# Attention backward on one core: two PSUM copies exchanged between ScalarE and VectorE

## The chip, the core and the metric

The kernel runs on one core of a Trainium2 chip. The metric is the device time of one execution in microseconds (us); less is better. The time before is 1711.55 us, the median of seven runs that lie between 1707.64 and 1726.95 us.

Five engines of the core work side by side, each through its own instructions in order: TensorE (PE; loading its weights is shown apart as PEld), VectorE (DVE), ScalarE (ACT), GpSimd (POOL) and SyncE (SP), which here only starts transfers. Matmul results land in PSUM, from which VectorE and ScalarE copy them to SBUF, the working memory.

## The reference

Two independent attention blocks, A and B, of the same shape; the kernel gives the forward output and all gradients of both.

```python
B, Sq, D = 8, 96, 640
H, Sk, Dh = 32, 512, 128
def _A_ref(x, k_cache, v_cache, wq, wo):
    q = (x @ wq).reshape(B, Sq, H, Dh).transpose(0, 2, 1, 3)
    scores = jnp.einsum("bhqd,bhkd->bhqk", q, k_cache) * (Dh ** -0.5)
    p = _softmax(scores, axis=-1)
    o = jnp.einsum("bhqk,bhkd->bhqd", p, v_cache)
    return o.transpose(0, 2, 1, 3).reshape(B, Sq, H * Dh) @ wo
...
out, vjp = jax.vjp(forward, A_x, A_k_cache, A_v_cache, A_wq, A_wo, B_x, ...)
return (out, *vjp(grad_out))
```

So for each block there are the output and dx, dK, dV, dwq and dwo. All tensors are bf16. One gradient matters here: dwo of a head is the head's attention output O, tokens by 128, transposed, times grad_out, tokens by 640, summed over all 768 tokens (8 batches of 96).

## The kernel before

There are 2 x 32 heads of 8 batches each: 512 steps of one head and one batch, called ticks here. A class `Emitter` collects small functions with a tick and a slot within the tick, sorts them and emits them in that order, so that the stages of several batches and heads are interleaved. A scheduler below it then arranges the instructions on each engine by its own estimates and by priorities, and puts in the waits; the order on an engine can therefore change when an instruction changes its engine. All PSUM tiles come from one pool of eight banks (`bank`, tag "bank"): a new tile waits until the tile that last held its bank has been read.

In a tick the pipeline holds several batches at different stages. In the order of the chain for one batch:

- c_s2a: scores S_ps = Q K^T (L298, TensorE) and their negative row maximum negm (L300, VectorE).
- c_s2b: E_sb = exp(S - max) with the row sums (L310, ScalarE; the read of the sums is an instruction of its own, ACTIVATION_READ_ACCUMULATOR).
- c_s3a, c_s3b: rinv (L320, VectorE) and P_sb (L329, POOL).
- c_s45: the transposes of P (L365), the O matmuls (L359), and the copies PT_sb (L378) and OD (L375), both ScalarE. OD holds O and dQ, transposed, for some heads.
- c_s4: dV_ps (L389) and its copy (L392, ScalarE).
- c_s5b, c_s6: prod (L407, POOL), dP_ps (L417), dl_ps (L419), and dS_sb (L421, VectorE), which reads both PSUM tiles.
- c_s7: dK_ps (L432) and its copy (L435, ScalarE).
- c_s8: the dQ matmuls (L340), which share a PSUM tile x_ps with the O matmuls, and the transposes of dS (L346) with the copy dST_sb (L348, VectorE).
- In half the ticks K is transposed on TensorE (kT_ps L285) and copied by VectorE (KT_pe L287).

In every eighth tick, and spread over its neighbours, stands the work of a head. Ahead of a head: pB (transposes of wo and wq), pC (Q and dO projections, L243), pD (the same in token order, n_ps L258, copied as Qnat_h and dOnat_h). Behind a head, ten ticks and more after it: qA(h, 1) brings dQ to token order, qA(h, 0) brings O to token order, qB makes dwo in two halves of 320 columns, and qD makes dwq for two heads together. gU adds a group's share to the output and to dx (o_ps L512).

The table HK gives the ticks: within a head's schedule qA1 stands at 17, qA0 at 18, and the halves of qB at 19 and 20. The table EV (L47) names the engine of each head-level copy, "act" for ScalarE or "dve" for VectorE; evac (L155) turns the name into an instruction, whose line in the profile is L157 on ScalarE and L160 (L162 with a scale) on VectorE. The change concerns the copies at the ends of qA and qB:

```python
# qA, which == 0
n_ps = bank([128, 8 * 128], BF16, "nat_ps")
for i in range(nt):
    nc.tensor.transpose(n_ps[:, i * 128:(i + 1) * 128], src[...], ident[:])
evac(EV["qA%d" % which], dst[...], n_ps[:, 0:nt * 128]...)
# qB
w_ps = bank([128, w], F32, "dwo_ps")
for t in range(TT):
    nc.tensor.matmul(w_ps[:], Onat[:, t, :], S["g_nat"][:, t, c0:c0 + w], ...)
evac(EV["qB%d" % di], dwo_sb[:, c0:c0 + w], w_ps[:])
```

Onat (the copy of O in token order, 128 x 768 in bf16) and dwo_sb (128 x 640 in bf16) have one buffer each. After the second half, dwo_sb is stored by a DMA that POOL issues (L474; in the last head SP).

Of the kernel before, what the change touches and what calls it, by code (L numbers as in the profile page):

```python
# [43 lines left out]

OFF = dict(ldk=-5, ldv=-3, kt=-3, vt=0, s2=3, s3=3, s4=4, s5=5, s6=6, s7=7, s8=8)
HK = dict(pA=-10, pA2=-9, pB=-3, pC0=[-2, 0], pC1=[-1, 0], pD1=1, pD0=2, qA0=18, qA1=17, qB=[19, 20], qD=[(18, 0, 2), (19, 2, 4), (21, 4, 5)])
EV = dict(pB0="act", pB1="dve", pC00="act", pC01="act", pC10="act", pC11="dve", pD0="dve", pD1="dve", qA0="dve", qA1="dve", qB0="act", qB1="act", qD="dve", gU="act")  # L47
GSPREAD0 = 9
PRIO_OFF = 2000
GSPREAD1 = 9  # L50
# [3 lines left out]
def build_block(tc, em, tick0, blk, x, kc, vc, wq, wo, g_all, out_all, dx, dk, dv, dwq, dwo, ident, ones, pools, HG=6, first=True, groups=None):  # L54
# [100 lines left out]
    def evac(eng, dst, src, sc=None):  # L155
        if eng == "act":
            nc.scalar.activation(dst, src, ACT.Identity, scale=(1.0 if sc is None else sc))  # L157
        else:
            if sc is None:
                nc.vector.tensor_copy(dst, src)  # L160
            else:
                nc.vector.tensor_scalar(dst, src, float(sc), None, op0=ALU.mult)  # L162
# [42 lines left out]
    def pB(h):  # L205
        def f():
# [4 lines left out]
            woT_h = hd.tile([128, DC * 128], BF16, name="woT_h", bufs=1)  # L211
            evac(EV["pB0"], woT_h[:], woT_ps[:])
            st["woT_h"] = woT_h
# [3 lines left out]
            wqT_h = hst.tile([128, D], BF16, name="wqT_h")  # L217
            evac(EV["pB1"], wqT_h[:], wqT_ps[:])
            st["wqT_h"] = wqT_h
# [7 lines left out]
    def pC(h, which, si):  # L227
        def f():
# [13 lines left out]
            for c in range(DC):  # L242
                nc.tensor.matmul(q_ps[:], lhs(c), rhsT[:, c, t0:t0 + w], start=(c == 0), stop=(c == DC - 1))  # L243
            evac(EV["pC%d%d" % (which, si)], dst[:, t0:t0 + w], q_ps[:], sc)
        return f

    def pD(h, which):
        def f():
# [4 lines left out]
            for b0 in range(0, B, 8):  # L253
                nb = min(8, B - b0)
                n_ps = bank([Sq, 8 * 128], BF16, "n_ps")
                for i in range(nb):
                    b = b0 + i
                    nc.tensor.transpose(n_ps[:, i * 128:(i + 1) * 128], src[:, b * Sq:(b + 1) * Sq], ident[:])  # L258
                evac(EV["pD%d" % which], dst[:, b0 * 128:(b0 + nb) * 128], n_ps[:, 0:nb * 128])
        return f  # L260
# [177 lines left out]
    def qA(h, which):  # L438
        def f():
# [11 lines left out]
            for t0 in range(0, TT, 8):  # L451
                nt = min(8, TT - t0)
                n_ps = bank([128, 8 * 128], BF16, "nat_ps")
                for i in range(nt):
                    nc.tensor.transpose(n_ps[:, i * 128:(i + 1) * 128], src[:, (t0 + i) * 128:(t0 + i + 1) * 128], ident[:])  # L455
                evac(EV["qA%d" % which], dst[:, t0:t0 + nt, :], n_ps[:, 0:nt * 128].rearrange("p (t d) -> p t d", d=128))
        return f

    def qB(h, di):
        def f():  # L460
# [8 lines left out]
            for t in range(TT):  # L469
                nc.tensor.matmul(w_ps[:], Onat[:, t, :], S["g_nat"][:, t, c0:c0 + w], start=(t == 0), stop=(t == TT - 1))  # L470
            evac(EV["qB%d" % di], dwo_sb[:, c0:c0 + w], w_ps[:])
            st["dwo_n"] += 1
# [269 lines left out]
```

## Time and profile before

| | |
|---|---|
| median of seven runs | 1711.55 us |
| the profiled execution | 1708.54 us |
| its span, first to last instruction | 1706.7 us |
| mean granted TensorE clock | 0.995 |
| DMA share, mean rate | nine tenths or more in most slices, 248 GB/s |

The profile shows one execution. "Busy" is the time in which an engine works on an instruction; a wait shows as idle time before an instruction, with the engine or transfer that ended it. Matmuls overlap in TensorE's pipeline and their ends are modelled, so that TensorE's busy time is not a measure of how dense its work is.

The load on the engines differs between the ticks of a head. The table shows busy time in four neighbouring ticks, cut at the starts of S_ps, around the copies of one head (its Onat copy starts at 311.48 us):

| stretch, us | length | VectorE busy | ScalarE busy | what of the head lies in it |
|---|---|---|---|---|
| 307.42 to 310.09 | 2.67 | 2.67 | 2.52 | dQnat, dOnat_h copies (VectorE) |
| 310.09 to 313.22 | 3.13 | 3.13 | 2.49 | Onat, Qnat_h copies (VectorE) |
| 313.22 to 315.21 | 1.99 | 1.59 | 1.69 | first dwo copy (ScalarE) |
| 315.21 to 318.02 | 2.81 | 1.71 | 2.81 | second dwo copy (ScalarE) |

The longest waits over the whole run: P_sb on POOL for rinv of VectorE 572.9 us, E_sb on ScalarE for negm of VectorE 206.1, rinv on VectorE for E_sb of ScalarE 121.1, dK_sb on ScalarE for dK_ps of TensorE 62.6. Idle time of an engine that nobody waits for costs nothing.

### The profile page before, as it was taken

How to read it: one execution, taken by the hardware profiler on the slowest of the kernel's cores; microseconds unless marked ns; L12 is line 12 of the kernel's file. 1: busy time of each engine (PE TensorE's matmuls, PEld its weight loads, DVE VectorE, ACT ScalarE, POOL GpSimd, SP SyncE). 2: the span in 40 equal slices, each digit the busy share in tenths (PEclk: the TensorE clock that was granted, in tenths of full speed). 3: DMA queues.
4: the chain of work that ended last, by engine and by line, in shares of the span. 5: the costliest groups of instructions: out<-in, count | busy, mean ns of one | idle time of the engine just before them, and what ended most of it. 6: DMA issues, size and time to landing. Idle time of an engine off the chain costs nothing.

```text
span 1706.7 us, 56912 instructions
## 1 busy us (share of the span) xinstructions
PE 1682.9 (99%) x22008; PEld 1347.3 (79%) x22008; DVE 1323.5 (78%) x3048; ACT 1383.5 (81%) x3518; POOL 1040.0 (61%) x1747
## 2 busy tenths in 40 slices
PE   8989999999999999999899999999999999999999
PEld 6878778778778778778778877887788778778876
DVE  6877678878788778788778876787788778778877
ACT  7988789868869869869668997997799679868974
POOL 4766566656647647657466765675566557656754
PEclk9999999999999999999899999999999999999999
DMA  9999999989989999989999999999999999999994
GB/s 265 259 243 257 257 226 290 261 205 251 273 204 268 267 216 273 265 215 239 273 255 267 284 250 247 251 260 252 216 271 249 255 225 267 252 235 237 271 237 138
DMA packets 602543, 423.58 MB, mean 248 GB/s; under 512 B 421472, under 2 KB 560096, under 8 KB 602272
## 3 DMA queue, kind: packets, MB, share of 16 engines
q1 hardware_dynamic: 548688, 242.60, 71.4%
q0 software_dynamic: 53584, 177.35, 32.3%
q8 instruction: 172, 2.82, 0.7%
q14 instruction: 99, 0.81, 0.1%
HBM read 161.09 MB, written 159.12 MB: 188 GB/s over the span
## 4 chain that ended last, share of the span: by engine, by line
PE 92%; DMA 2%; ACT 2%; DVE 1%; issue 1%; POOL 0%; SPq 0%; DVEq 0%; ACTq 0%; POOLq 0%
PE o_ps L512 12%; PE q_ps L243 12%; PE dwo_ps L470 6%; PE dV_ps L389 6%; PE dK_ps L432 6%; PE dP_ps L417 6%; PE S_ps L298 6%; PE dwq_ps L490 6%; PE x_ps L340 5%; PE x_ps L365 5%; PE dst_ps L346 5%; PE x_ps L359 5%; PE kT_ps L285 3%; PE n_ps L258 3%; PE nat_ps L455 3%
## 5 line engine op out<-in xcount | busy, mean ns | idle before, releaser
L329 POOL TENSOR_SCALAR P_sb<-E_sb,rinv 96x512 bf16<-96x512 bf16 x512 | 352.3, 688 | 581.1 <-DVE rinv L320 572.9
L310 ACT ACTIVATE E_sb<-S_ps,negm 96x512 bf16<-96x512 f32 x512 | 356.4, 696 | 211.1 <-DVE negm L300 206.1
L421 DVE SCALAR_TENSOR_TENSOR dS_sb<-dP_ps,dl_ps,P_sb 96x512 bf16<-96x512 f32 x512 | 382.9, 748 | 64.1 <-PE dl_ps L419 48.1
L300 DVE TENSOR_REDUCE negm<-S_ps 96x1 f32<-96x512 f32 x512 | 347.5, 679 | 54.2 <-PE S_ps L298 51.3
L435 ACT ACTIVATE dK_sb<-dK_ps 128x512 bf16<-128x512 f32 x512 | 308.2, 602 | 68.9 <-PE dK_ps L432 62.6
L392 ACT ACTIVATE dV_sb<-dV_ps 128x512 bf16<-128x512 f32 x512 | 317.3, 620 | 0.0
L378 ACT ACTIVATE PT_sb<-x_ps 128x384 bf16<-128x384 bf16 x512 | 258.9, 506 | 0.0
L512 PEld LDWEIGHTS <-OD 128*128 128x128 bf16 x1536 | 132.2, 98 | 99.6
L398 POOL DMA_DIRECT2D out_dram<-dV_sb x256 | 194.9, 761 | 11.7 <-issue 8.3
L398 POOL DMA_DIRECT2D out_dram<-dK_sb x256 | 195.0, 762 | 8.8 <-issue 4.5
L389 PE MATMUL dV_ps<-dOnat_h,P_sb 96*128 96x128 bf16 x2048 | 198.6, 219 | 0.8 <-DVE dOnat_h L160 0.6
L432 PE MATMUL dK_ps<-Qnat_h,dS_sb 96*128 96x128 bf16 x2048 | 198.3, 219 | 0.0
L417 PE MATMUL dP_ps<-VT,dOT_h 128*96 128x512 bf16 x512 | 196.6, 384 | 1.7 <-DMA VT<-V_sb 1.7
L407 POOL TENSOR_TENSOR prod<-OD,dOT_h 128x96 bf16<-128x96 bf16 x512 | 184.0, 359 | 13.8 <-ACT OD L375 12.6
L348 DVE COPY dST_sb<-dst_ps 128x384 bf16<-128x384 bf16 x512 | 177.2, 346 | 7.4 <-PE dst_ps L346 6.1
L320 DVE RECIPROCAL rinv<-rowsum 96x1 f32<-96x1 f32 x512 | 79.5, 155 | 127.3 <-ACT E_sb L310 121.1
L375 ACT ACTIVATE OD<-x_ps 128x192 bf16<-128x192 f32 (+1 forms) x515 | 173.7, 337 | 4.0 <-PE x_ps L340 3.8
L365 PE MATMUL x_ps<-ident,P_sb 96*128 96x96 bf16 x2048 | 172.3, 205 | 1.2 <-POOL P_sb L329 0.8
L346 PE MATMUL dst_ps<-ident,dS_sb 96*128 96x96 bf16 x2048 | 172.4, 206 | 0.5 <-DVE dS_sb L421 0.5
L359 PE MATMUL x_ps<-PT_sb,V_sb 128*128 128x96 bf16 x2048 | 172.4, 206 | 0.4 <-ACT PT_sb L378 0.4
L340 PE MATMUL x_ps<-dST_sb,K_sb 128*128 128x96 bf16 x2048 | 171.0, 206 | 0.4 <-ACT PT_sb L378 0.4
L340 PEld LDWEIGHTS <-K_sb 128*128 128x128 bf16 x2048 | 131.8, 98 | 24.8 <-issue 0.8
(83 smaller groups left out, 3728.7 us busy)
## 6 DMA issues: line engine op xcount, KB each, us to landing
out_dram<-dV_sb POOLq DMA_DIRECT2D x256, 256.0 KB, 5.1
out_dram<-dK_sb POOLq DMA_DIRECT2D x256, 256.0 KB, 5.3
K_sb<-in_A_k_cache_dram SPq DMA_DIRECT2D x128, 256.0 KB, 4.9
V_sb<-in_A_v_cache_dram SPq DMA_DIRECT2D x128, 256.0 KB, 4.8
K_sb<-in_B_k_cache_dram SPq DMA_DIRECT2D x128, 256.0 KB, 5.3
V_sb<-in_B_v_cache_dram SPq DMA_DIRECT2D x128, 256.0 KB, 4.9
out_dram<-dwo_sb POOLq DMA_DIRECT2D x63, 160.0 KB, 4.9
out_dram<-dwq_sb POOLq DMA_DIRECT2D x31, 320.0 KB, 5.6
```

The lines of the kernel that those rows point to most:

```text
L300: nc.vector.tensor_reduce(negm[:], S_ps[:], axis=AX.X, op=ALU.max, negate=True)
L310: nc.scalar.activation(E_sb[:], st["S_ps"][:], ACT.Exp, bias=st["negm"][:], scale=1.0, accum_out=rowsum[:])
L329: pinned(nc.gpsimd.tensor_scalar(P_sb[:], st["E_sb"][:], st["rinv"][:], 0.0, op0=ALU.mult, op1=ALU.add))
L340: nc.tensor.matmul(dQT_ps, st["K_sb"][:, c, :], st["dST_sb"][:, c * Sq:(c + 1) * Sq], start=(c == 0), stop=(c == KC - 1))
L389: nc.tensor.matmul(dV_ps[:, c * 128:(c + 1) * 128], P_sb[:, c * 128:(c + 1) * 128], hs["dOnat_h"][:, b * 128:(b + 1) * 128], start=True, s ...
L392: nc.scalar.activation(SB[(blk, h, b // 2, "v")][:, b % 2], dV_ps[:], ACT.Identity, scale=1.0)
L398: pinned(nc.gpsimd.dma_start(dst[b - 1:b + 1, h].rearrange("b (p c) d -> p b (c d)", c=KC), SB.pop((blk, h, b // 2, which))[:]))
L417: nc.tensor.matmul(dP_ps[:], hs["dOT_h"][:, tok], st["VT"], start=True, stop=True)
L421: nc.vector.scalar_tensor_tensor(dS_sb[:], dP_ps[:], dl_ps[:, 0:1], st["P_sb"][:], op0=ALU.subtract, op1=ALU.mult)
L432: nc.tensor.matmul(dK_ps[:, c * 128:(c + 1) * 128], dS_sb[:, c * 128:(c + 1) * 128], hs["Qnat_h"][:, b * 128:(b + 1) * 128], start=True, s ...
L435: nc.scalar.activation(SB[(blk, h, b // 2, "k")][:, b % 2], dK_ps[:], ACT.Identity, scale=1.0)
L512: nc.tensor.matmul(o_ps[:], src[:, t * 128:(t + 1) * 128], rhs, start=(hh == 0), stop=(hh == groups[g] - 1))
```

## The change

Two entries of the table EV change. The copy of O in token order, qA0, goes from VectorE to ScalarE; the copy of the second half of dwo, qB1, goes from ScalarE to VectorE. Each is made 64 times, once per head. Computation, tiles, buffers and transfers stay.

```diff
-EV = dict(pB0="act", ..., qA0="dve", qA1="dve", qB0="act", qB1="act", qD="dve", gU="act")
+EV = dict(pB0="act", ..., qA0="act", qA1="dve", qB0="act", qB1="dve", qD="dve", gU="act")
```

More of the change, by code (lines that the diff above doesn't have):

```diff
@@ L46 @@
 HK = dict(pA=-10, pA2=-9, pB=-3, pC0=[-2, 0], pC1=[-1, 0], pD1=1, pD0=2, qA0=18, qA1=17, qB=[19, 20], qD=[(18, 0, 2), (19, 2, 4), (21, 4, 5)])
-EV = dict(pB0="act", pB1="dve", pC00="act", pC01="act", pC10="act", pC11="dve", pD0="dve", pD1="dve", qA0="dve", qA1="dve", qB0="act", qB1="act", qD="dve", gU="act")
+EV = dict(pB0="act", pB1="dve", pC00="act", pC01="act", pC10="act", pC11="dve", pD0="dve", pD1="dve", qA0="act", qA1="dve", qB0="act", qB1="dve", qD="dve", gU="act")
 GSPREAD0 = 9
```

## The prediction

> **What bounds the kernel now.** First the page, for the engine that is busiest and for the chain that ended last; then the groups with their shapes, for the price of a copy on either engine; then the timeline of one head on ScalarE, VectorE and TensorE.
>
> ```profile
> PE 1682.9 (99%) x22008; PEld 1347.3 (79%) x22008; DVE 1323.5 (78%) x3048; ACT 1383.5 (81%) x3518; POOL 1040.0 (61%) x1747
> ...
> PE 92%; DMA 2%; ACT 2%; DVE 1%; issue 1%; POOL 0%; SPq 0%; DVEq 0%; ACTq 0%; POOLq 0%
> ```
>
> TensorE is the wall: 99% busy, and 92% of the chain runs over it. No copy costs time by itself; it costs only where TensorE waits for it. But 99% hides small stalls, because the ends of matmuls are modelled and cover the gap behind them. So I read the starts. Undisturbed, successive matmuls of the same width start a fixed step apart (in the timeline 42 ns for 96 columns, 56 for 128, 136 for 320, 216 for 512). Each start-to-start gap of all 22,008 matmuls, less that step for the earlier one, gives **about 68 us of stall** over 1701 us. That is all that any evacuation edit can win. Cut at the starts of S_ps (L298), which gives eight ticks per head, four stalls above 60 ns recur at fixed places: dwo_ps (L470) in 25 heads, 4.6 us; dl_ps (L419) just before it in 21 heads, 3.8 us; the P transposes (x_ps L365) two ticks later in 23 heads, 3.5 us; the dQ matmuls (x_ps L340) one tick on in 23 heads, 3.9 us. **Sum 15.8 us.** One such head, the one whose O copy starts at 311.48 us, shows all four. TensorE:
>
> ```profile
> 312.08 0.42 PE L417 MATMUL dP_ps<-VT,dOT_h 128*96 128x512 bf16 x1
> 312.48 0.16 PE L419 MATMUL dl_ps<-ones,prod 128*96 128x1 bf16 x1
> 312.68 0.70 PE L470 MATMUL dwo_ps<-g_nat,Onat 128*128 128x320 bf16 x4
> ```
>
> A 512-column matmul should be followed after 0.22 us; dl_ps comes after 0.40 (0.185 late), dwo_ps after another 0.20 where 0.03 would do (0.167 late). Who ended just then stands in VectorE's and ScalarE's rows:
>
> ```profile
> 310.88 0.68 DVE L300 TENSOR_REDUCE negm<-S_ps 96x1 f32<-96x512 f32 x1
> 311.48 0.55 DVE L160 COPY Onat<-nat_ps 128x768 bf16<-128x768 bf16 x1
> 311.94 0.68 DVE L160 COPY Qnat_h<-n_ps 96x1024 bf16<-96x1024 bf16 x1
> ...
> 318.00 0.16 DVE L320 RECIPROCAL rinv<-rowsum 96x1 f32<-96x1 f32 x1 [0.99 <-ACT E_sb L310]
> ```
>
> ```profile
> 310.42 0.60 ACT L392 ACTIVATE dV_sb<-dV_ps 128x512 bf16<-128x512 f32 x1
> 311.66 0.68 ACT L310 ACTIVATE E_sb<-S_ps,negm 96x512 bf16<-96x512 f32 x1 [0.64 <-DVE negm L300]
> 312.24 0.19 ACT L310 ACTIVATION_READ_ACCUMULATOR E_sb<-S_ps,negm 96x1 f32 x1
> ...
> 316.86 0.45 ACT L157 ACTIVATE dwo_sb<-dwo_ps 128x320 bf16<-128x320 f32 x1
> 317.17 0.70 ACT L310 ACTIVATE E_sb<-S_ps,negm 96x512 bf16<-96x512 f32 x1
> ```
>
> dl_ps starts 0.05 us after the accumulator read ends (312.43): it waits for the PSUM bank of the scores. dwo_ps starts 0.06 after Qnat ends (312.62): the bank of n_ps. And Qnat is late because Onat stands in front of it, in a stretch of VectorE without one gap from 307.9 to 314.5, in which ScalarE idles 0.64 us. Later it is the other way round: at 316.86 the second dwo copy holds E_sb, whose negm ended at 316.73, while VectorE idles 0.99 us for it. The other two stalls hang on that: x_ps L365 starts at 316.99 just after P_sb lands (0.143 late), x_ps L340 at 318.89 just after dS_sb (0.161 late), both downstream of late E_sb.
>
> **Part by part.** The prices come from the nearest groups:
>
> ```profile
> L378 ACT ACTIVATE PT_sb<-x_ps 128x384 bf16<-128x384 bf16 x512 | 258.9, 506 | 0.0
> L157 ACT ACTIVATE woT_h<-woT_ps 128x640 bf16<-128x640 bf16 x64 | 46.5, 726 | 0.0
> L157 ACT ACTIVATE dwo_sb<-dwo_ps 128x320 bf16<-128x320 f32 x128 | 56.5, 442 | 4.6 <-PE dwo_ps L470 1.9
> ...
> L160 DVE COPY Onat<-nat_ps 128x768 bf16<-128x768 bf16 x64 | 34.8, 544 | 0.0
> L162 DVE TENSOR_SCALAR dwq_sb<-dwq_ps 128x512 bf16<-128x512 f32 x64 | 44.0, 688 | 30.3 <-PE dwq_ps L490 30.3
> L160 DVE CAST dOT_h<-q_ps 128x256 bf16<-128x256 f32 x64 | 26.6, 415 | 7.8 <-PE q_ps L243 7.8
> ```
>
> *Onat on ScalarE.* Two rows give a line: (726-506)/256 = 0.86 ns a column, so 768 columns take 726 + 128 x 0.86 = **836 ns**. Ends: 726 (the narrower copy) and 871 (726 scaled by width). In the compiled order it stands between dV_sb and E_sb, exactly in the gap: back-to-back ScalarE rows overlap by about 0.09, so it runs 310.93 to 311.77 and E_sb starts at 311.68, 0.02 late. The same subtraction in every head gives 0.02 in 20 heads, room of 0.25 to 2.1 us in all others but one, where it pushes a copy by 0.8 us (at 845 us). dP_ps now takes the bank that Onat frees, at 311.82, ahead of 312.08. At 871 ns the 20 heads lose 0.05 each, 1 us.
>
> Here the Trainium skill speaks against the change: "ScalarE: Activation LUTs", Rules for kernel authors, wants simple elementwise work on VectorE, which it calls up to about 3 times faster per element in bf16. By that the copy takes up to 3 x 544 = 1.63 us, E_sb is pushed 0.81 in 20 heads and about 0.36 in 18 more (room 0.45): 23 us of delay. By the rows the ratio out of PSUM is 1.5 (726 against 478 ns for woT_h and wqT_h, both 128x640). I take the rows.
>
> *VectorE without Onat.* Qnat runs 311.48 to 312.16, and dl_ps, which in the new order waits for that bank, is free at 312.30. dwo_ps instead waits for the bank of the scores: accumulator read 312.45, start 312.50, where an unstalled TensorE arrives at 312.33. So 0.17 of 0.35 us stays. In the 20 heads of this pattern the compiler also splits the first dwo group around S_ps as 1+5 in place of 4+2, puts V's matmuls (L359) behind dK_ps and E_sb ahead of dK_sb. S_ps comes some 0.55 us sooner; with VectorE ahead, negm starts near 313.5 (was 313.86) and E_sb near 314.3 (was 315.13). P_sb then comes well before L365 asks: its 0.143 goes. dK_sb becomes later by about 0.35 us; its store has a tick of room.
>
> *Second dwo half.* On VectorE: (688-415)/256 = 1.07 ns a column, 415 + 64 x 1.07 = **483 ns** (ends 415 and 688). In 47 heads it stands behind negm and delays dST_sb by 0.35 to 0.44; TensorE reads dST_sb over a tick later, and the 0.99 us of idle before rinv hides it, at 688 ns too. In 11 heads it stands ahead of negm and pushes it by 0.16: 1.8 us if nothing hides that, 4 us at 688. ScalarE's E_sb can start behind negm, which itself comes earlier: near 316.55, was 317.17. dS_sb must come 0.48 earlier to clear L340 (0.161, plus 0.32 by which TensorE is now ahead); it comes some 0.6 earlier. That stall goes. The store of dwo (POOL, L474) waits for VectorE in place of ScalarE; in this head it issues at 317.98 behind another store anyway. SP and POOL keep their order.
>
> *Sum.* 15.8 (four stalls) - 3.6 (dwo_ps on E_sb, 21 x 0.17) - 1.8 (11 heads) - 0.8 (one head) = **9.6 us** won. Engine totals: ScalarE +53.5 - 28.3 = +25 us, VectorE -34.8 + 30.9 = -4, more work in all, and none of it counts. The profiled execution took 1708.54 us (span 1706.7 and 1.8 around it), which gives 1698.9; it lies 3.0 below the median of the runs, 1711.55, on which I put the forecast: **1702 us**.
>
> **Rivals.** *B, the softmax chain keeps the gain.* S_ps, negm, E_sb, rinv, P_sb follow one another; E_sb still waits for negm where it stalls dwo_ps. If the two later stalls only move, 8.4 - 3.6 - 2.6 = 2.2 us are left: 1709.4. For it: rinv's wait for E_sb (121 us) and E_sb's for negm (206 us) are among the longest; saturated stretches tend to hand a stall on. Against it: the second move shortens this chain just there.
> *C, slower: ScalarE holds E_sb.* It is in order, so a long Onat copy delays every softmax. Place: the 20 tight heads, then the 18 with 0.45 room. Loss begins when 20 pushes eat 9.6 us, at a copy of 0.836 + 0.48 = 1.3 us; at 1.63 us it is 1711.55 + 22.7 - 9.6 = 1724.7. For it: ScalarE is already the busiest behind TensorE. Against it: no row of 640 columns or fewer comes near.
> *That nothing moves* falls away: the compiled order has all 64 Onat copies on ScalarE and 64 dwo copies on VectorE.
>
> **How the numbers follow.** A: 0.48, 1696 to 1703. B: 0.40, 1703 to 1712. C: 0.12, from 1712. What a measurement can tell from no change is about 0.5%, 8.6 us, so A is faster, B the same, C counts as slower, since most of it lies beyond 1720. The range goes from all four stalls gone with nothing left (1695) to a little into C (1714); 0.05 below, 0.10 above.
>
> **What would show it.** Onat on ScalarE near 836 ns and E_sb's wait for negm shorter than 206 us, since the copy fills it. dwo_sb on VectorE near 483. dl_ps following dP_ps by 0.22 us; dwo_ps 0.05 behind the accumulator read. In the third tick no stall before L365, in the fourth none before L340. Wrong: a copy beyond 1 us, new TensorE gaps before dP_ps (Onat's bank) or before dV_ps, or the same stall total under other names.

## The result, and the profile after

The changed kernel takes 1706.92 us (median of 27 runs, 1695.34 to 1722.99) where the kernel before, run beside it, takes 1713.5 (64 runs, 1698.04 to 1731.51). The ratio is **0.9972, 95% interval 0.9952 to 0.9992**: a gain of 0.28%, about 4.8 us, which is under the bound of 0.5% and half of the 0.56% that was forecast. The ratio counts only executions within 1.5% of the fastest one of the same kernel, the medians count all, so that they lie further apart (6.6 us). A second set (e9, below) gave 0.9967 (0.9939 to 0.9995).

The profiled execution of the changed kernel is, however, longer than that of the kernel before: 1716.32 against 1708.54 us, spans 1714.5 and 1706.7. That is no contradiction. With the count of the prediction (start to start of all 22,008 matmuls, less the step for their width), cut at 0.4 us into short and long stalls:

| one execution of | span, us | short stalls | long stalls (number) | the rest |
|---|---|---|---|---|
| before | 1706.7 | 50.1 | 17.8 (15) | 1638.8 |
| changed | 1714.5 | 46.6 | 29.0 (19) | 1638.9 |
| changed, second set (e9) | 1726.1 | 45.1 | 42.0 (28) | 1639.0 |

What is left when both kinds are taken off is the same by the way of counting: it is the steps of the same 22,008 matmuls, and the 5.5 us ahead of the first and from the start of the last, which are alike too. The long stalls, by time mostly waits for loads, differ from one execution to the next by more than the whole effect. The short ones lie at the same places in both traces of the changed kernel and fell from 50.1 to 46.6 or 45.1.

Even so they are not all the kernel's own. In 17.1 us of the execution before, and in 23.9 and 20.5 us of the other two, the trace shows a granted clock of 0.50; there every step is longer, and these steps make up about 5.9, 9.8 and 6.6 us of the short stalls. **At full clock the short stalls fell from 44.2 to 36.8 and 38.5 us, by 7.4 and 5.7 us**; the ratios are worth 4.8 and 5.7 us. Of the short stalls, those from 60 ns up in the ticks of a head (after the first head, without q_ps and o_ps, for which the traces of e1 to e4 and e13 lack 166 matmul records each) fell from 27.6 to 24.2 us, at full clock from 25.3 to 20.3 and 21.5.

The page of the changed kernel, engines and chain, answers to the first lines shown of before:

```profile
PE 1679.3 (98%) x22008; PEld 1346.2 (79%) x22008; DVE 1329.1 (78%) x3048; ACT 1406.6 (82%) x3518; POOL 1040.3 (61%) x1747
...
PE 88%; ACT 4%; DMA 4%; issue 2%; DVE 1%; POOL 0%; SPq 0%; DVEq 0%; ACTq 0%; POOLq 0%
```

ScalarE is up by 23.1 us (predicted 25), VectorE by 5.6 (predicted -4; the durations of its instructions added up do fall, by 3.2, but the page counts time in which two overlap once, and fewer overlap now), and 4% of the chain now runs over ScalarE, where it was 2%. The groups with their shapes (count | busy us, mean ns | idle before) give the prices of the two moves:

```profile
L157 ACT ACTIVATE Onat<-nat_ps 128x768 bf16<-128x768 bf16 x64 | 52.5, 820 | 2.9 <-PE nat_ps L455 2.9
...
L160 DVE CAST dwo_sb<-dwo_ps 128x320 bf16<-128x320 f32 x64 | 30.8, 481 | 1.2 <-PE dwo_ps L470 0.6
```

820 and 481 ns stand against 836 and 483 predicted. Out of PSUM the O copy costs ScalarE 820/544 = 1.5 times what it cost VectorE, not up to 3 times, and the slower case that hung on this is gone. The waits (us in total, times, longest):

```profile
ACT E_sb L310 <- DVE negm L300: 191.6, 220, 6.9
DVE rinv L320 <- ACT E_sb L310: 100.1, 237, 0.9
```

Both are shorter than before (206.1 and 121.1); for the first this was forecast. Now the timeline of the head that was shown, whose O copy now starts at 310.23. TensorE, first tick:

```profile
311.39 0.38 PE L417 MATMUL dP_ps<-VT,dOT_h 128*96 128x512 bf16 x1
311.61 0.17 PE L419 MATMUL dl_ps<-ones,prod 128*96 128x1 bf16 x1
311.83 0.30 PE L470 MATMUL dwo_ps<-g_nat,Onat 128*128 128x320 bf16 x1
```

dl_ps follows dP_ps by 0.22 us: its stall is gone. dwo_ps should follow 0.03 later and comes after 0.22. Fourth tick, the kernel before first (TensorE, VectorE, ScalarE):

```profile
318.50 0.38 PE L285 MATMUL kT_ps<-ident,K_sb 128*128 128x128 bf16 x4
318.89 0.33 PE L340 MATMUL x_ps<-dST_sb,K_sb 128*128 128x96 bf16 x4
...
318.08 0.75 DVE L421 SCALAR_TENSOR_TENSOR dS_sb<-dP_ps,dl_ps,P_sb 96x512 bf16<-96x512 f32 x1
...
318.52 0.52 ACT L378 ACTIVATE PT_sb<-x_ps 128x384 bf16<-128x384 bf16 x1
```

There L340 starts 0.06 after dS_sb ends (318.83), while PT_sb of this run ends only later (319.04). The changed kernel:

```profile
317.41 0.39 PE L285 MATMUL kT_ps<-ident,K_sb 128*128 128x128 bf16 x4
317.81 0.33 PE L340 MATMUL x_ps<-dST_sb,K_sb 128*128 128x96 bf16 x4
317.98 0.34 PE L346 MATMUL dst_ps<-ident,dS_sb 96*128 96x96 bf16 x4
```

Four transposes of 56 ns fill 0.22 us; L340 comes after 0.40, still 0.18 late. ScalarE and VectorE tell who ended 0.05 us before:

```profile
310.23 0.82 ACT L157 ACTIVATE Onat<-nat_ps 128x768 bf16<-128x768 bf16 x1
311.00 0.68 ACT L310 ACTIVATE E_sb<-S_ps,negm 96x512 bf16<-96x512 f32 x1
311.58 0.19 ACT L310 ACTIVATION_READ_ACCUMULATOR E_sb<-S_ps,negm 96x1 f32 x1
...
315.91 0.68 ACT L310 ACTIVATE E_sb<-S_ps,negm 96x512 bf16<-96x512 f32 x1
316.50 0.19 ACT L310 ACTIVATION_READ_ACCUMULATOR E_sb<-S_ps,negm 96x1 f32 x1
316.59 0.58 ACT L435 ACTIVATE dK_sb<-dK_ps 128x512 bf16<-128x512 f32 x1
317.07 0.32 ACT L375 ACTIVATE OD<-x_ps 128x192 bf16<-128x192 f32 x1
317.28 0.49 ACT L378 ACTIVATE PT_sb<-x_ps 128x384 bf16<-128x384 bf16 x1
```

```profile
315.14 0.68 DVE L300 TENSOR_REDUCE negm<-S_ps 96x1 f32<-96x512 f32 x1
315.74 0.48 DVE L160 CAST dwo_sb<-dwo_ps 128x320 bf16<-128x320 f32 x1
...
316.72 0.16 DVE L320 RECIPROCAL rinv<-rowsum 96x1 f32<-96x1 f32 x1 [0.24 <-ACT E_sb L310]
316.85 0.75 DVE L421 SCALAR_TENSOR_TENSOR dS_sb<-dP_ps,dl_ps,P_sb 96x512 bf16<-96x512 f32 x1
```

dwo_ps waits for the accumulator read (ends 311.77, starts 311.83). L340 no longer waits for dS_sb, which ends at 317.60; it starts 0.04 after PT_sb ends (317.77). PT_sb is the last of three copies that stand without a gap behind E_sb, and E_sb started 0.09 after its negm ended, just as the dV copy ahead of it ended. Over all heads the instruction that ends 0.05 us before each stalled L340 was dS_sb in 20 of 23 before, and is PT_sb in 20 of 21 now.

### The profile page after: what moved, and what is told of

It is laid out like the page before. It is cut to its first block, busy times and chain, and to the rows that moved or that the text cites. A ratio compares the mean times of both kernels' runs of the same rounds, so it can differ in the third digit from the quotient of the medians.

```text
span 1714.5 us, 56974 instructions
## 1 busy us (share of the span) xinstructions
PE 1679.3 (98%) x22008; PEld 1346.2 (79%) x22008; DVE 1329.1 (78%) x3048; ACT 1406.6 (82%) x3518; POOL 1040.3 (61%) x1747
## 4 chain that ended last, share of the span: by engine, by line
PE 88%; ACT 4%; DMA 4%; issue 2%; DVE 1%; POOL 0%; SPq 0%; DVEq 0%; ACTq 0%; POOLq 0%
PE q_ps L243 12%; PE o_ps L512 12%; PE dwq_ps L490 6%; PE dwo_ps L470 6%; PE dV_ps L389 6%; PE dK_ps L432 6%; PE S_ps L298 6%; PE dP_ps L417 6%; PE x_ps L340 5%; PE x_ps L365 5%; PE dst_ps L346 5%; PE x_ps L359 5%; PE kT_ps L285 3%; PE n_ps L258 3%; PE nat_ps L455 2%; DMA VT<-V_sb 2%
## 5 line engine op out<-in xcount | busy, mean ns | idle before, releaser
L310 ACT ACTIVATE E_sb<-S_ps,negm 96x512 bf16<-96x512 f32 x512 | 351.1, 686 | 197.2 <-DVE negm L300 191.6
L435 ACT ACTIVATE dK_sb<-dK_ps 128x512 bf16<-128x512 f32 x512 | 302.2, 590 | 64.6 <-PE dK_ps L432 60.0
L392 ACT ACTIVATE dV_sb<-dV_ps 128x512 bf16<-128x512 f32 x512 | 311.6, 609 | 0.0
L378 ACT ACTIVATE PT_sb<-x_ps 128x384 bf16<-128x384 bf16 x512 | 253.1, 494 | 0.0
L346 PE MATMUL dst_ps<-ident,dS_sb 96*128 96x96 bf16 x2048 | 172.6, 206 | 0.5 <-DVE dS_sb L421 0.5
L340 PE MATMUL x_ps<-dST_sb,K_sb 128*128 128x96 bf16 x2048 | 171.2, 206 | 0.6 <-ACT PT_sb L378 0.2
L375 ACT ACTIVATE OD<-x_ps 128x192 bf16<-128x192 f32 (+1 forms) x515 | 167.9, 326 | 4.0 <-PE x_ps L340 3.9
L340 PEld LDWEIGHTS <-K_sb 128*128 128x128 bf16 x2048 | 131.5, 98 | 24.6 <-issue 0.9
```

The lines of the kernel that those rows point to most:

```text
L310: nc.scalar.activation(E_sb[:], st["S_ps"][:], ACT.Exp, bias=st["negm"][:], scale=1.0, accum_out=rowsum[:])
L340: nc.tensor.matmul(dQT_ps, st["K_sb"][:, c, :], st["dST_sb"][:, c * Sq:(c + 1) * Sq], start=(c == 0), stop=(c == KC - 1))
L392: nc.scalar.activation(SB[(blk, h, b // 2, "v")][:, b % 2], dV_ps[:], ACT.Identity, scale=1.0)
L435: nc.scalar.activation(SB[(blk, h, b // 2, "k")][:, b % 2], dK_ps[:], ACT.Identity, scale=1.0)
```

## The experiments

The theories: the rest of the gain was held by ScalarE's full queue in that head; by the one move giving back what the other won; or by the softmax chain negm, E_sb, rinv, dS_sb, negm, which runs once per tick over VectorE and ScalarE (E_sb starts at 311.00, 313.58 and 315.91, 2.58 and 2.33 us apart; TensorE, on time, takes 2.41 and 2.60 for the ticks that begin with S_ps at 311.96 and 314.37). All edits are made in the changed kernel unless it is said otherwise. Recurring short stalls (60 ns to 0.4 us, after the first head) in us, with the heads at the places that matter in brackets and a dash for at most 0.3 us. The last column leaves out the stretches with a granted clock of 0.50, which differ between executions (it rests on slightly other steps, worth up to 0.2 us, in e3 and e13 up to 0.9). The expectations count with other cuts (e1: 42.5 and 39.1 us for the 50.1 and 46.6 above; e5 to e7: 15.8 for the 24.2 of the changed kernel), so compare differences and not levels.

| run | dwo_ps | dl_ps | P transp. | dQ L340 | S_ps, fourth tick | dst_ps L346 | all but q_ps, o_ps | at full clock |
|---|---|---|---|---|---|---|---|---|
| before | 4.6 (25) | 3.8 (21) | 3.5 (23) | 3.9 (23) | 0.3 | - | 27.6 | 25.3 |
| changed | 5.2 (26) | - | 0.6 | 3.9 (21) | 2.1 (14) | - | 24.2 | 20.3 |
| e1 | 5.0 | - | 0.6 | 7.3 (21) | 2.1 | - | 25.3 | 25.8 |
| e2 | 4.6 | 3.4 | 3.1 | 3.0 (21) | 1.9 | - | 25.7 | 25.8 |
| e3 | 4.8 | - | 0.6 | 3.8 (23) | 2.1 | - | 22.4 | 21.3 |
| e4 | 5.0 | - | 0.6 | 8.1 (24) | 2.0 | - | 26.3 | 26.0 |
| e5 | 3.8 | - | - | 3.8 (22) | 2.0 | - | 20.9 | 21.0 |
| e6 | 4.8 | - | - | 3.7 (20) | 1.9 | - | 21.9 | 20.5 |
| e9 | 5.5 | - | 0.6 | 3.9 (19) | 1.9 | - | 24.0 | 21.5 |
| e10 | 3.7 | - | - | 3.0 (20) | 2.1 | - | 22.3 | 22.0 |
| e11, e14 | - | - | - | 0.4, 1.1 | - | 4.1 (18), 4.7 (20) | 8.4, 11.5 | 7.9, 9.2 |
| e12, e16 (in before) | - | - | - | 3.1, 3.8 | - | 2.9, 2.9 (14, fourth tick after) | 11.3, 13.1 | 9.9, 9.5 |
| e13, e15 | - | - | - | 0.8, 0.9 | - | 0.9 (4), 1.3 (5) | 6.2, 7.2 | 3.9, 5.1 |

**Each move alone (e1, e2).** From the kernel before, one entry each:

```diff
-qA0="dve"
+qA0="act"
```

```diff
-qB1="act"
+qB1="dve"
```

> Only the O copy goes to ScalarE; both dwo halves stay there. Measure: the sum of TensorE stalls up to 0.4 us, counted over the starts of all matmuls (before 42.5 us, after 39.1). Theory 1, ScalarE's queue is full: with 53 us more on ScalarE and nothing taken off, the stall of dl_ps (3.8 us) goes, but the P transposes (x_ps L365, 3.5 us before, 0.6 after) wait again and the dQ matmuls (x_ps L340, 3.9) wait at least as much; small stalls 42 to 46 us, time within 0.3% of before or slower. Theory 2, all of the gain comes from relieving VectorE: stalls about 39, time as after, 0.3% less than before.

> Only the second half of dwo goes to VectorE. Theory 1, ScalarE's queue is full: dl_ps and dwo_ps keep their 3.8 and 4.6 us, but the P transposes and the dQ matmuls lose most of their 7.4 us, because E_sb no longer stands behind that copy; small stalls 36 to 39 us, time 0.2 to 0.4% less than before, at least as good as both moves. Theory 2, relief of VectorE is what counts: VectorE is loaded more, no stall falls, small stalls 42 or more, time as before.

e1: 1716.43 us, ratio to before 1.0002 (0.9976 to 1.0028). e2: 1715.87, 1.0017 (0.9996 to 1.0039). No time can be told from no change. The stalls say more. The O copy alone clears dl_ps and the P transposes, but doubles the stall before the dQ matmuls to 7.3 us; the second dwo copy alone clears next to nothing, and the second move's part in the change is to bring 7.3 back to 3.9. At full clock neither alone has fewer stalls in sum than before (25.8 and 25.8, against 25.3), while both together have 20.3. At the places that are late in more than ten heads of one of the two kernels e1 wins 2.0 us and e2 1.0, both together 5.1. So neither takes from the other; each clears what the other opens or leaves. In e1 and e2, too, PT_sb ends 0.05 us before L340 in 20 of 21 heads: either move alone is enough to change what L340 waits for.

**The other halves (e3, e4).** All of dwo on VectorE; then the first half there in place of the second:

```diff
-qB0="act", qB1="dve"
+qB0="dve", qB1="dve"
```

```diff
-qB0="act", qB1="dve"
+qB0="dve", qB1="act"
```

> On top of the change the first half of dwo goes to VectorE too, which takes 28 us off ScalarE in the tick before the stall. Theory 1, ScalarE's queue without a gap holds PT_sb and so the bank that the dQ matmuls (x_ps L340) wait for: that stall falls from 3.9 to under 1 us, the one of S_ps in the same tick (2.1 us, 14 heads) falls too; dwo_ps keeps its 5 us, since there E_sb waits for negm; small stalls 33 to 36 us, time 0.2 to 0.4% less than after. Theory 3, the chain S_ps, negm, E_sb, rinv sets these stalls, whatever ScalarE carries: they stay, small stalls 39 or more.

> The first half of dwo goes to VectorE in place of the second, with the O copy on ScalarE. ScalarE carries the same as in the change, but its relief comes one tick earlier and the second copy again stands ahead of E_sb two ticks on. Theory 1: the P stall (x_ps L365) comes back in part, the dQ stall (x_ps L340) stays near 4 us; small stalls 38 to 43 us. Theory 3: as after, 39 us, because the chain and not the place of the copy decides.

e3: 1712.65, 0.9998 (0.997 to 1.0027); e4: 1710.93, 0.9984 (0.995 to 1.0017). e3 takes 0.44 us off ScalarE in the tick where it has no gap, and L340 stays 3.8 us late in all. ScalarE now idles there, and E_sb of the fourth tick starts 0.09 after its negm ends (307.19):

```profile
304.95 0.68 ACT L310 ACTIVATE E_sb<-S_ps,negm 96x512 bf16<-96x512 f32 x1 [0.24 <-DVE negm L300]
...
307.28 0.68 ACT L310 ACTIVATE E_sb<-S_ps,negm 96x512 bf16<-96x512 f32 x1
...
306.51 0.68 DVE L300 TENSOR_REDUCE negm<-S_ps 96x1 f32<-96x512 f32 x1
```

ScalarE's queue alone is not the reason, then; e3 does, however, give VectorE the copy that it takes from ScalarE. e4 is late by 8.1 us at L340, much as e1 was by 7.3: both leave the second half ahead of E_sb on ScalarE, and that is the place where it costs.

**The order on ScalarE (e5, e6).** The dK copy behind PT_sb; then OD and PT_sb raised in the scheduler's priority (PT_sb shown; the OD copy gets the same line):

```diff
-S8=10, S7=20, S5=30
+S8=10, S7=35, S5=30
```

```diff
-nc.scalar.activation(PT_sb[:], PT_ps, ...)
+with tc.high_priority(2 * PRIO_OFF):
+    nc.scalar.activation(PT_sb[:], PT_ps, ...)
```

> On top of the change the stage that makes dK is emitted behind the one that makes PT_sb, so that ScalarE runs E_sb, OD, PT_sb, dK_sb, dV_sb in every tick in place of E_sb, dK_sb, OD, PT_sb, dV_sb. Nothing is added or taken off. Theory 1, the dQ stall (x_ps L340) of the changed kernel is the bank that PT_sb frees, and PT_sb is late because it stands behind E_sb and dK_sb in ScalarE's order: PT_sb ends about 0.45 us sooner, and that stall falls from 3.9 to under 1 us; the P transposes are asked for 0.2 us sooner and may wait up to 2 us in return; recurring stalls (0.06 to 0.4 us, over all heads) fall from 15.8 by 1 to 3 us. Theory 3, the chain from S_ps over negm to E_sb is too long for these ticks: the stall moves to another matmul of the same tick, total as in the change.

> On top of the change OD and PT_sb get a higher priority, which puts them ahead of dK_sb in the first and second tick of each head's end, but not in the third, where dK_sb still stands ahead of PT_sb. Theory 1: the dQ stall of the fourth tick keeps its 3.9 us, since the PT_sb that it waits for has not moved against dK_sb; recurring stalls 15 to 16 us. Theory 3: the same. A fall below 2 us would speak against both: then the copies one and two ticks earlier set it.

e5: 1709.7, 0.9994 (0.9959 to 1.003); e6: 1710.56, 1.0007 (0.9978 to 1.0036). e6 leaves L340 at 3.7 us, as expected. In e5 L340 keeps its 3.8 us too; in sum nothing is won at full clock (21.0 against 20.3), since n_ps is now late in 42 heads, 3.0 us, behind PT_sb. ScalarE and TensorE of e5 in a head of this kind:

```profile
307.99 0.48 ACT L378 ACTIVATE PT_sb<-x_ps 128x384 bf16<-128x384 bf16 x1
308.36 0.59 ACT L435 ACTIVATE dK_sb<-dK_ps 128x512 bf16<-128x512 f32 x1
```

```profile
308.60 0.39 PE L285 MATMUL kT_ps<-ident,K_sb 128*128 128x128 bf16 x4
309.00 0.33 PE L340 MATMUL x_ps<-dST_sb,K_sb 128*128 128x96 bf16 x4
```

PT_sb ends at 308.47, half a microsecond ahead of need, and L340 starts at 309.00 all the same: 0.05 after dK_sb, which ends at 308.95. In all 22 heads it is dK_sb now. L340 does not read dK_sb or PT_sb, so this is a wait for a bank. In both orders L340 waits for the copy that ends the stretch OD, PT_sb and dK behind E_sb; that copy is another one, its end comes at about the same time.

**One bank less, and the O copy twice (e7, e8).** These measure how dear a missing bank and a longer ScalarE copy are:

```diff
-ps=P(name="ps", bufs=8, space=PSUM)
+ps=P(name="ps", bufs=7, space=PSUM)
```

```diff
+dup = hd.tile([128, TT, 128], BF16, name="Odup", bufs=1)
+evac("act", dup[:, t0:t0 + nt, :], n_ps[:, 0:nt * 128]...)
 evac(EV["qA%d" % which], dst[...], n_ps[:, 0:nt * 128]...)
```

> On top of the change seven PSUM banks in place of eight, each used as before. If the recurring stalls are waits for a bank (dwo_ps for that of the scores, x_ps L340 for that of PT_sb, S_ps L298 for that of the scores), they come at more places and grow: recurring stalls 60 us or more in place of 15.8, time at least 3% more than before. If they are waits for data (dST_sb, KT, Onat), a bank less changes little: under 25 us, time within 1%.

> On top of the change ScalarE makes the O copy twice, the second into a tile that nobody reads, which makes the step cost about 1.6 us in place of 0.82. It prices the rival of a too long copy. Prediction of the sum: E_sb is pushed by 0.75 us in 20 heads and by 0.3 us in 18 more, 20 us in all if nothing hides it: dwo_ps's stall grows from 0.2 to 0.9 us in the 20 heads; time 0.8 to 1.4% more than after. If ScalarE's slack is larger than counted: under 0.4% more.

e7: 1746.61 us in one run, 1.9% above the 1713.83 of before beside it, with short stalls of 82.3 in place of 46.6 us. That is less than the 3% expected, but more than the 1% set for waits for data. The stalls also move: dwo_ps and L340 are on time in their ticks, while nat_ps in the last tick of a head is late by 11.6 us, with eight banks by 4.1. Such gaps from a missing bank are in line with the Trainium skill ("Perfetto Trace Analysis", Optimization Strategy), which takes the same gap coming back on the engine that should be saturated as a possible sign that SBUF or PSUM is short for the next tile. e8: 1711.13, 0.9994 (0.9961 to 1.0028). Stalls up to 1.2 us counted, dwo_ps is late by 10.0 us in 26 heads (5.2 with one copy) and dP_ps by 8.2 in 20, where it had none: 13.0 us at the two places, where 20 were expected, and 0.2% in the ratios, which their intervals don't tell from nothing. Two copies take 1.64 us, just what the forecast's slower case assumed for one; by the two places its 22.7 us were priced too high.

**The changed kernel again, and e3 with e5 (e9, e10).**

> The changed kernel once more, unaltered, against the kernel before. If its gain is the sum of the recurring stalls (27.6 to 24.2 us; 3.4 us with the small ones), the ratio comes out near 0.998 (0.996 to 1.000), and a second profile shows the same recurring stalls at the same places: dwo_ps about 5 us, the dQ matmuls (x_ps L340) about 4, S_ps about 2, none at dl_ps, under 1 at the P transposes. Should the stalls sit at other places in a second execution, the counting by places says nothing of the program.

> The changed kernel with both dwo halves on VectorE and the copy of dK after PT_sb (the two edits with the lowest stall counts, 22.4 and 20.9 us). If the two add, recurring stalls come to about 19 us, some 5 us (0.3%) under the changed kernel's 24.2, and the ratio to before is near 0.995. By the theory of the softmax chain (the dQ matmuls wait for the end of ScalarE's run behind E_sb, whatever stands last in it, and E_sb is paced by negm) the stall before the dQ matmuls stays at 3.5 to 4 us on dK_sb. By the theory that ScalarE's load in that tick is the cause, it falls under 2 us, since ScalarE has 0.44 us less to do in that head.

e9: 1709.09 against 1716.55, 0.9967 (0.9939 to 0.9995). The gain is there again, and every recurring stall at its place. e10 (the diffs of e3 and e5): 1709.88, 0.9992 (0.9966 to 1.0017); 22.3 us, at full clock 22.0, no better than either edit by itself. L340 is late by 3.0 us, on dK_sb. They don't add.

**The chain made shorter (e11 to e16).** The maximum is only a shift of the softmax. Taken over the first 128 keys in place of all 512 it leaves the softmax as it is, rounding apart, as long as no exponent overflows, and the reduction takes 0.28 in place of 0.68 us, while every ScalarE instruction stays. e11 and e14 do it in the changed kernel, e12 and e16 in the one before; e13 and e15 add the diff of e3.

```diff
-nc.vector.tensor_reduce(negm[:], S_ps[:], axis=AX.X, op=ALU.max, negate=True)
+nc.vector.tensor_reduce(negm[:], S_ps[:, 0:128], axis=AX.X, op=ALU.max, negate=True)
```

> The changed kernel with negm taken over the first 128 of the 512 keys of a row only (a smaller shift; the softmax does not depend on the shift, but the exponent is no longer bounded by the row's own maximum). The reduction falls from 0.68 to about 0.28 us, so each round of the chain negm, E_sb, rinv, dS_sb is 0.4 us shorter, while ScalarE has the same work. Theory of the chain: the stalls that the change left or opened, dQ matmuls 3.9, S_ps 2.1 and dwo_ps 5.2 us, fall to under 1.5 us each, the recurring ones in all from 24.2 to 10 to 15 us, and the time falls by 8 to 14 us, ratio to before 0.991 to 0.995. Theory that ScalarE's queue is simply full there: E_sb starts earlier only where it waited for negm, the dQ matmuls' stall stays above 3 us, and the time falls by under 4 us.

> The same shorter reduction in the kernel before the change. Theory of the chain: VectorE is no longer packed round the O copy, so Qnat_h and E_sb come in time and all four stalls of the prediction (dwo_ps 4.6, dl_ps 3.8, P transposes 3.5, dQ matmuls 3.9 us) fall to under 1.5 us each; then the change is worth nothing any more, and this run and the changed kernel with the same reduction lie within 0.3% of each other. If the stalls of the kernel before stay and the changed kernel's go, the change would be worth its forecast 9.6 us once the chain is shorter.

> The changed kernel with negm over 128 keys and the first dwo half on VectorE too, so that both the softmax chain (0.4 us a round) and ScalarE (0.44 us in that head) are lighter. With the shorter chain alone the recurring stall before the dQ matmuls fell from 3.9 to 0.4 us, but 4.1 us came up one step later, at the transposes of dS (dst_ps, 18 heads, on ScalarE's dV_sb); with the lighter ScalarE alone the dQ stall stayed at 3.8. Theory that both limits lie side by side, each alone holding some 4 us: with both lighter the stall before dst_ps falls under 1.5 us as well and nothing takes its place, recurring stalls (without q_ps and o_ps) from 8.4 to under 6 us, ratio to before about 0.990 (0.987 to 0.994). Theory that the chain alone was the limit and dst_ps is an order of its own: dst_ps stays at 3 to 4 us on dV_sb.

In the table, e13 is without q_ps and o_ps.

| run | ratio to before, 95% | short stalls, us | long stalls, us |
|---|---|---|---|
| e11 changed, short negm | 0.9916 (0.9876 to 0.9955) | 25.0 | 22.6 |
| e12 before, short negm | 0.9936 (0.9908 to 0.9964) | 33.4 | 51.0 |
| e13 changed, short negm, all dwo on VectorE | 0.997 (0.9931 to 1.001) | 26.1 | 29.1 |
| e14 as e11 | 0.9988 (0.9965 to 1.0012) | 31.5 | 31.6 |
| e15 as e13 | 0.99 (0.9865 to 0.9936) | 27.1 | 27.7 |
| e16 as e12 | 0.9958 (0.993 to 0.9987) | 33.1 | 36.2 |

In e11 dwo_ps and S_ps are clear and L340 is late in one head only. But 4.1 us come up at the transposes of dS right behind it. ScalarE and TensorE of e11 in a head of this kind:

```profile
417.22 0.55 ACT L378 ACTIVATE PT_sb<-x_ps 128x384 bf16<-128x384 bf16 x1
417.59 0.67 ACT L392 ACTIVATE dV_sb<-dV_ps 128x512 bf16<-128x512 f32 x1
```

```profile
417.89 0.33 PE L340 MATMUL x_ps<-dST_sb,K_sb 128*128 128x96 bf16 x4
418.31 0.33 PE L346 MATMUL dst_ps<-ident,dS_sb 96*128 96x96 bf16 x4
```

L340 is on time, since PT_sb ended at 417.77. L346 should follow by 0.17 us and comes after 0.42, 0.05 behind the end of dV_sb (418.26), the next copy of the same run. So ScalarE's load stands beside the chain as a second limit of about the same size. e13 and e15 make both lighter, and that stall goes too (0.9 and 1.3 us), with nothing in its place: of the two readings that e13 was to tell apart, two limits side by side is the right one. e12 fits: with both dwo halves on ScalarE the shorter chain leaves 3.1 us at L340, on PT_sb. Its expectation that all four stalls would go was wrong there.

Two cautions. The shorter reduction also takes 171 us of busy time from VectorE (1329.1 to 1158.2 busy) and lets the compiler order some instructions anew, so e11 is not the chain alone. And the times scatter more than their intervals say:

> Negm over 128 keys in the changed kernel, once more, on one chip with the next two. If the time follows the small stalls (25.0 us, against 50.1 before the change), the ratio to before lies at 0.985 to 0.993; if the 0.9916 of the first time came from the chip or the hour, it lies near the 0.997 of the run with all of dwo on VectorE.

> The same with the first dwo half on VectorE too. Small stalls 26.1 us, recurring ones 6.2: by the stalls the same time as the run ahead within 0.2%, ratio to before 0.985 to 0.993. If it stays near 0.997 while the run ahead is near 0.992, the second dwo copy on VectorE costs some 8 us that the starts of the matmuls don't show.

> Negm over 128 keys in the kernel before, small stalls 33.4 us, 8.4 more than with the change. If the change is worth its forecast once the chain is shorter, this run lies 0.4 to 0.6% above the first of this call; if it is worth nothing there, within 0.2%.

On one chip e11's kernel was ahead of e13's, on the next it was behind, and the two intervals of the same kernel (e11, e14) don't touch; the ratios of e13 and e14 lie above the 0.987 to 0.994 and 0.985 to 0.993 expected by the stalls, e15 within. The medians of all executions lie closer: 0.9932 and 0.9971 (e11, e14), 0.9927 and 0.9963 (e12, e16), 0.9950 and 0.9916 (e13, e15). The stalls by place came back in all of them. e14 had 6.5 us more short stalls than e11, of which 4.4 lie in stretches at a clock of 0.50.

In the kernel before, the shorter chain gained 0.64 and 0.42%, both clear of noise. Together with the change, the ratios of e11 and e15 are clear of 1 and those of e13 and e14 are not. All six gain less than the 17 to 25 us (1.0 to 1.5%) by which the short stalls fell in the profiled executions; which of the three kernels is fastest is open, and so is where the rest went. What the change is worth with the shorter chain is up to 0.3% by the times, of either sign, and 2.0 and 0.3 us by the recurring stalls at full clock (e12 against e11, e16 against e14). e15's version beats the kernel before in both sets by its middle values (0.99 and 0.997), but it has no guard against overflow for inputs whose maximum lies beyond the first 128 keys and is much larger; it is an experiment and no replacement.

## Why the prediction was half right

- *The wall is TensorE, and only its late starts can be won*: right as far as it was tried. The steps of its matmuls and the 5.5 us around them make 1638.8 of 1706.7 us. That this rest was the same in every trace follows from the count and proves nothing; that 7.4 and 5.7 us of short stalls went where the times gained 4.8 and 5.7 does speak for it.
- *Prices of the two copies*: right to 2%.
- *dl_ps clear, dwo_ps held by the accumulator read*: right in place; the term of 3.6 us measured 5.2, in 26 heads at 0.20 us in place of 21 at 0.17.
- *The P transposes clear*: right but for 0.6 us.
- **The step that failed: "dS_sb must come 0.48 earlier to clear L340 ...; it comes some 0.6 earlier. That stall goes."** Two things in it were wrong. The smaller one is the size: against TensorE dS_sb was to come 0.28 us earlier (0.6 less 0.32) and came 0.14 earlier, where 0.16 was needed (in this head it ended at 317.60 and L340 on time would have needed 317.58). By dS_sb alone L340 would now start 0.02 late, 0.4 us over 20 heads. The larger one is the wait: the stall stayed, 3.9 us of 3.9. In the new order L340 is given another bank, one that ScalarE frees: among L340's waits in the compiled order those on ScalarE rise from 279 to 320 and those on VectorE fall from 174 to 164. That could have been read beforehand. The prediction followed the old releaser downstream and never asked which copy would hold the new bank, nor added up ScalarE's run: E_sb from 315.91, then dK, OD and PT_sb to 317.77. e5 shows that the end of this run holds it whatever stands there, e3 that lighter ScalarE work alone doesn't free it, e11 that a shorter chain does but meets ScalarE's load one copy on, and e13 and e15 that with both lighter the stall goes and nothing takes its place.
- *Nothing new elsewhere, but for 1.8 us in 11 heads and 0.8 in one*: about that size, elsewhere. S_ps in the fourth tick rose by 1.8 us, held by E_sb in 14 heads, and o_ps by 0.7. (dwo_ps two ticks later rose by 0.8 as well, but in stretches at a clock of 0.50.)
- *The sum*: the four stalls went from 15.8 to 9.7 us, by 6.1; over all recurring stalls, q_ps and o_ps with them, 28.6 became 25.8, at full clock 26.6 became 22.0. So 4.6 us were won, in the trace of e9 3.2, where 9.6 were forecast. Of the 5.0 between 9.6 and 4.6, L340 makes 3.9, dwo_ps 1.6 and the P transposes 0.6, and 1.1 less came up elsewhere than was allowed for. A fifth recurring stall was overlooked: nat_ps in the last tick of a head, 4.0 us in 44 heads, held by the dOnat_h copy on VectorE in 39; the change left it at 4.1. The rival "the softmax chain keeps the gain", at 2.2 us, had the chain right, but only one of its two stalls stayed, and that one hangs on ScalarE's load as well; the truth lies between it and the forecast.

## What to carry to other kernels

When a change moves the order of tiles through a shared PSUM pool, ask anew which tile's bank each stalled matmul is given, and follow the engine that frees it to the end of its queue; that the old releaser comes earlier is not enough. Where VectorE and ScalarE pass a chain to and fro in the time of one TensorE tick, both the chain and each engine's load can be the limit within a few tenths of a microsecond, and relieving one hands the stall to the next copy. Count start-to-start gaps, and take out the long ones and the stretches at a lower clock, before a profile of one execution is set against another.

## What the runs showed that was not expected

The long stalls of TensorE took 10.8 to 51.0 us in single executions of these kernels (table above; 10.8 in e5, which is why its span was only 1688.1 us), against the 4.8 us that the change won. Some of them come with a slower clock; in e5 none did, the clock stood at 1.00 from 6.0 us to the end. The windows of the kernel before, around three waits for a load, of 2.97, 1.04 and 1.25 us, that end at 827.40, 831.82 and 833.78 (the stretch; length, then busy time and instructions of TensorE, its weight loads, VectorE, ScalarE and GpSimd; granted clock, DMA share, GB/s):

```profile
826.00:832.00 6.00, 3.56 (x38) 3.02 (x39) 2.50 (x6) 2.46 (x6) 2.17 (x4) 0.69 1.19 246
...
834.00:836.00 2.00, 2.00 (x21) 1.72 (x20) 1.46 (x3) 0.68 (x2) 0.00 (x0) 0.50 1.09 410
836.00:838.00 2.00, 2.00 (x18) 1.50 (x17) 0.88 (x4) 1.83 (x6) 1.44 (x3) 0.50 1.06 350
```

The clock stands at 0.50 from 828.2 to 838.5, for over 4 us after the last of the waits, and a 512-column matmul takes 0.63 us in place of 0.38 in the records. In the count such steps are stalls as well, which is why they were taken out above.

A run of one kernel on another chip can lie 0.7% from the first in its ratio to before (0.9916 and 0.9988), outside both 95% intervals; by the medians of all executions it is 0.4%.
